# Batch 0's output product made whole instead of from half-size block products, with a new table of ranks

## The chip, the cores and the metric

One core of a Trainium2 chip runs the whole program. The metric is the time of one execution on the device, in microseconds. The engines are named as the profile names them: PE (TensorE matmul), PEld (its weight loads), DVE (VectorE), ACT (ScalarE), POOL (GpSimd), SP (SyncE, which issues every DMA here).

## What is computed

Eight batches of banded attention (8 heads, 576 positions, head size 64) feed a gated layer with spatial mixing. Cut to what matters:

```python
attn = softmax(scale * q @ k.T, masked to a band of 32, or of 128 at every 4th place)   # per head
x    = (attn @ v) with the heads side by side                     # 576 x 512 per batch
h    = relu(x @ w_in);  u, v = h[..., :512], h[..., 512:]
v_n  = (v - mean(v)) / sqrt(var(v) + 1e-6)
v_s  = einsum('ts,bsd->btd', w_spatial, v_n) + b_spatial
out  = (u * v_s) @ w_out                                          # the output product
```

## The kernel before

**Numbers in two parts.** Operands of the large products are split into a high and a low part (names ending in `h` and `l`), and a product is three passes: high by high, high by low, low by high (`PASSES`, line 272). A product of 128x128 by 128x288 over 512 inputs is then 4 x 3 = 12 matmuls.

**Stages of a batch.** `unit` (line 452) makes the scores of two head pairs, 24 small matmuls on parts of the array (line 465 in the trace, 48 records each), the softmax on DVE, ACT and POOL, and three transposes on PE (line 513) that ACT copies out (line 516). `weighted` (line 521) multiplies by the values (line 541, small matmuls too). `features_in` (line 574) splits the result. `v_tile` (line 592) makes the v half (lines 610 and 624) and normalises it. `gate` (line 697) makes the spatial product (lines 707 to 709) and multiplies it by u (DVE, line 714).

**Half-size block products.** The u half (from batch 1 on; batch 0's is made whole by `upper`, line 677, since `FU` is 1 at line 674) and the output product (in every batch) are not made whole. Both operands are cut in 2x2 blocks, and seven products of blocks replace eight: `differences` (line 803) makes differences of right-hand blocks on POOL (line 817), `factor` (line 771) splits seven right-hand blocks into high and low (ACT, line 790; DVE, line 276 through the helper `sub`), `summed` (line 735) makes sums and differences of the weight blocks once (POOL, lines 743 and 745; DVE, lines 748 to 754; ACT, line 765; DVE again through `sub`), and `piece` (line 845) makes each of the seven products in two halves `m` (6 matmuls each, line 827) and adds them up on DVE (line 868, or an ACT copy, line 870, for the first). So a batch's output product is 7 x 2 x 6 = 84 matmuls, and a whole one would be 8 x 12 = 96.

**The order of the work** is set while the program is built. Every function above is a generator that yields what it needs and the engine it wants next; `Timeline` (line 26) holds them with a rank each, keeps a modelled time of every engine, and at each step issues the instruction whose modelled start plus a small share of its rank is least (`run`, line 102). Small matmuls late in the program may be held back by up to 0.5 (`HOLD`, line 40) unless the one before was small too. The ranks come from formulas in the batch loop plus the table `shift` (line 926). `warm` (line 886) fills PE with dummy matmuls (line 891) whenever the modelled time is under 30 and nothing else is ready. Engines then run their queues strictly in that order.

**Start.** SP loads in the order of the list `first` (line 912). Each of the eight chunks of `w_in` and four of `w_out` arrives in 64-bit form and is converted by `weight` (line 296): ACT, four DVE steps, and a last sum made on PE (lines 331 to 333, then an ACT copy), on POOL or on DVE, as the table `ways` says (line 900).

Of the kernel before, what the change touches and what calls it, by code (L numbers as in the profile page):

```python
# [25 lines left out]
class Timeline:  # L26
# [13 lines left out]
    HOLD, HELD = 0.5, 0.5  # L40

# [23 lines left out]
    def start(self, s):  # L65
# [21 lines left out]
        s.wished = start + self.HOLD if small and not self.tiled else 0.0  # L87
# [14 lines left out]
    def run(self):  # L102
        W = 0.05
        while self.strands:
            best = None
            for s in list(self.strands):
                start = self.start(s)
                if start is None:
                    continue
                key = max(start, s.wished) + (W if start > 60 else 0.05) * s.rank[0]  # L110
                if best is None or key < best[2] - 1e-9:
                    best = (start, s, key)
# [31 lines left out]
def tile_banded_attention_gated_moe(  # L144
# [151 lines left out]
    def weight(key, hi, lo, dtype, how):  # L296
# [23 lines left out]
        tl.add(-0.15 + key[-1] * 0.01, rounded(hi, g, ("hi", *key)))  # L320
# [353 lines left out]
    FU = 1  # L674
# [58 lines left out]
    def summed(kind, i):  # L733
# [37 lines left out]
    def factor(b, kind, name, source):  # L771

        def needs(i):
            if len(name) == 1:
                return [("diff", b, kind, int(name), i)] + [("part", b, kind, "2", i)] * (name == "4")
            return [("g", b, *source(i))] + [("diff", b, kind, 2, i)] * (name == "22")

        yield needs(0)
        if kind == "u":
            yield [("fac", b - 1, "o", n) for n in ("11", "21", "1", "2", "3", "22", "4")]  # L780
        yield "fac"
        for i in range(2):
# [11 lines left out]
            if kind == "o" and name in ("3", "22", "4"):  # L794
# [89 lines left out]

    def warm():
# [14 lines left out]
    ways = ((POOL, PE, DVE, PE), (PE, PE, PE, PE), (PE, PE, DVE, PE))  # L900
    halves = {}
    for half in (1, 0):
        cols = slice(half * NF, half * NF + NF)
        for c in range(NC):
# [4 lines left out]
            r = -1.72 + 0.11 * c if half else -2.6 + 0.02 * c  # L909
# [4 lines left out]
        heads_in(0, 1, 1, NU), heads_in(0, 0, 1, NU), halves[1, 2], heads_in(0, 3), spatial_in(4), values_in(0, 0),  # L914
        halves[1, 3], halves[0, 3], halves[0, 2], values_in(0, 1), halves[1, 1], outs[2],
# [5 lines left out]
    for c in range(NC):  # L921
        tl.add(-1.46 + 0.36 * c, weight(("wo", c), wo[0][:, c, :], wo[1][:, c, :], w_out.dtype, ways[2][c]))
    for c in range(5):
        tl.add(1.56 if c < 4 else -0.79, spatial(c))
    tl.add(-0.15, bias())
    shift = {
        ("differences", 0): 0.6,
        ("differences", 1): 0.07,
        ("differences", 2): -0.22,
        ("differences", 3): 0.46,  # L930
        ("factor", 0): 0.18,
        ("factor", 1): 0.18,
        ("factor", 2): -0.33,
        ("factor", 3): -0.03,
        ("factor", 4): -0.26,
# [5 lines left out]
        ("factor", 10): -0.3,  # L941
        ("features_in", 0): -0.23,
        ("features_in", 1): 0.15,
        ("features_in", 2): -0.06,
# [3 lines left out]
        ("gate", 2): 0.07,  # L948
# [7 lines left out]
        ("piece", 0): 1.19,  # L956
# [3 lines left out]
        ("piece", 5): -0.72,  # L960
        ("piece", 6): -0.3,
        ("piece", 7): 0.07,
        ("piece", 8): 0.66,
# [3 lines left out]
        ("piece", 12): -0.11,  # L967
        ("piece", 14): 0.1,
        ("piece", 16): -0.37,
        ("piece", 17): -0.1,  # L970
# [4 lines left out]
        ("piece", 22): -0.52,  # L975
# [13 lines left out]
        ("values_in", 1): 0.3,  # L989
        ("values_in", 2): 0.15,  # L990
        ("values_in", 3): 0.01,
        ("weighted", 0): -0.21,
        ("weighted", 1): -0.52,
# [3 lines left out]
    def put(rank, strand):  # L997

        turn = turns[strand.__name__] = turns.get(strand.__name__, -1) + 1
        tl.add(rank + (shift.get((strand.__name__, turn), 0.0) if b else 0.0), strand)  # L1000

    for b in range(B):
        turns = {}
        AO, AS = (-0.7, 0.7) if b == 1 else (0.15, 0.65)
# [19 lines left out]
        for n, (name, source) in enumerate(  # L1024
            (("11", far(0, 0)), ("21", far(1, 0)), ("1", far(0, 0)), ("2", far(0, 0)), ("3", far(0, 1)), ("22", far(1, 1)), ("4", far(1, 0)))
# [4 lines left out]
        for i in range(2):  # L1030
            put(b + 0.75 + 0.01 * i, differences(b, "o", i))
# [92 lines left out]
```

## Time and profile before

| | |
|---|---|
| runs | 550.97, 550.05, 547.73 us; median 550.05 |
| the profiled execution | 547.6 us, with a span of 545.8 us (the rest, 1.8 us, lies around the span) |
| mean granted TensorE clock | 0.999 of full speed |
| PE busy | 536.9 us, 98% of the span |
| DVE busy | 437.6 us, 80% |
| ACT, POOL busy | 306.8 us, 56%; 213.8 us, 39% |

How to read it: the busy time of PE is the union of its matmul records, whose ends are modelled, so that the spacing of their starts tells more than their durations. A start that comes late shows in the idle time before it and in what released it. The profiled execution is the fastest of the four; the sums of the prediction are made against it.

### The profile page before, as it was taken

How to read it: one execution, taken by the hardware profiler on the slowest of the kernel's cores; microseconds unless marked ns; L12 is line 12 of the kernel's file. 1: busy time of each engine (PE TensorE's matmuls, PEld its weight loads, DVE VectorE, ACT ScalarE, POOL GpSimd, SP SyncE). 2: the span in 40 equal slices, each digit the busy share in tenths (PEclk: the TensorE clock that was granted, in tenths of full speed). 3: DMA queues.
4: the chain of work that ended last, by engine and by line, in shares of the span. 5: the costliest groups of instructions: out<-in, count | busy, mean ns of one | idle time of the engine just before them, and what ended most of it. 6: DMA issues, size and time to landing. Idle time of an engine off the chain costs nothing.

```text
span 545.8 us, 18357 instructions
## 1 busy us (share of the span) xinstructions
PE 536.9 (98%) x7591; PEld 488.1 (89%) x7591; DVE 437.6 (80%) x1036; ACT 306.8 (56%) x939; POOL 213.8 (39%) x255
## 2 busy tenths in 40 slices
PE   9998999999999999999999999999999999999997
PEld 7666789989999899988999999989999899989996
DVE  5888968999957898489957998489957999479836
ACT  4777796555654555556464655556464565454312
POOL 3320275453517163434427163343417163353140
PEclk9999999999999999999999999999999999999999
DMA  8999551201563144411464134521454134201002
GB/s 235 256 175 328 168 124 53 85 11 45 128 139 125 44 133 90 125 67 56 112 131 138 44 106 95 133 80 49 118 118 150 45 116 91 63 12 44 34 1 87
DMA packets 97447, 56.66 MB, mean 104 GB/s; under 512 B 78290, under 2 KB 87506, under 8 KB 97364
## 3 DMA queue, kind: packets, MB, share of 16 engines
q1 hardware_dynamic: 97364, 55.50, 38.1%
q8 instruction: 59, 0.97, 0.8%
q14 instruction: 24, 0.20, 0.1%
HBM read 46.04 MB, written 9.44 MB: 102 GB/s over the span
## 4 chain that ended last, share of the span: by engine, by line
PE 95%; ACT 2%; DMA 1%; issue 1%; DVE 1%; SPq 0%
PE bank L827 32%; PE bank L707 19%; PE bank L610 16%; PE bank L541 6%; PE bank L465 6%; PE bank L891 4%; PE bank L513 3%; PE bank L624 2%; PE bank L686 2%; PE bank L709 2%; PE bank L708 2%; DMA kqv<-in_vw_dram 1%; PE bank L331 1%; ACT p L493 1%; PE bank L332 0%
## 5 line engine op out<-in xcount | busy, mean ns | idle before, releaser
L868 DVE TENSOR_TENSOR ur<-ur,bank 128x288 f32<-128x288 f32 x210 | 87.3, 447 | 27.1 <-PE bank L827 26.8
L790 ACT CAST fac<-ur 128x288 fp32r<-128x288 f32 x112 | 46.2, 430 | 78.4 <-DVE ur L714 42.2
L707 PE MATMUL bank<-wth,vnh 128*128 128x288 f32 x256 | 76.5, 299 | 0.0
L276 DVE TENSOR_TENSOR fac<-ur,fac 128x288 fp32r<-128x288 f32 x112 | 60.5, 549 | 19.1 <-ACT fac L790 18.9
L707 PE MATMUL bank<-wth,vnl 128*128 128x288 f32 x256 | 75.6, 295 | 0.0
L707 PE MATMUL bank<-wtl,vnh 128*128 128x288 f32 x256 | 75.6, 295 | 0.0
L817 POOL TENSOR_TENSOR ur<-ur,ur 128x288 f32<-128x288 f32 x64 | 55.3, 874 | 44.4 <-DVE ur L714 34.0
L493 ACT ACTIVATE p<-p,nm 128x64 f32<-128x64 f32 x192 | 64.5, 338 | 12.5 <-DVE nm L487 10.1
L508 POOL TENSOR_TENSOR p<-p,rv 128x384 f32<-128x384 f32 x48 | 40.7, 850 | 77.1 <-DVE rv L506 61.0
L646 POOL TENSOR_TENSOR rs<-rs,halfneg 128x1 f32<-128x1 f32 (+1 forms) x40 | 27.9, 698 | 91.2 <-DVE rs L644 91.1
L827 PE MATMUL bank<-fac,woh 128*128 128x288 f32 x256 | 53.4, 298 | 0.1
L610 PE MATMUL bank<-wih,xl 128*128 128x512 f32 x128 | 50.1, 392 | 1.8 <-issue 1.8
L817 POOL TENSOR_TENSOR raw<-raw,raw 128x288 f32<-128x288 f32 x42 | 43.4, 1040 | 19.3 <-DVE fac L276 16.4
L610 PE MATMUL bank<-wih,xh 128*128 128x512 f32 x128 | 50.4, 394 | 0.0
L610 PE MATMUL bank<-wil,xh 128*128 128x512 f32 x128 | 50.3, 393 | 0.0
L707 PEld LDWEIGHTS bank<-wth,vnh 128*128 128x128 f32 x256 | 48.2, 188 | 0.4
L707 PEld LDWEIGHTS bank<-wth,vnl 128*128 128x128 f32 x256 | 48.1, 188 | 0.2 <-issue 0.2
L707 PEld LDWEIGHTS bank<-wtl,vnh 128*128 128x128 f32 x256 | 48.2, 188 | 0.0
L714 DVE SCALAR_TENSOR_TENSOR ur<-ur,bank 128x288 f32<-128x288 f32 x64 | 27.9, 448 | 21.1 <-PE bank L709 20.5
L827 PEld LDWEIGHTS bank<-fac,woh 128*128 128x128 f32 x256 | 42.2, 189 | 2.6 <-ACT raw L568 0.4
L827 PE MATMUL bank<-fac,o 128*128 128x288 f32 x288 | 44.0, 297 | 0.0
L827 PEld LDWEIGHTS bank<-fac,o 128*128 128x128 f32 x288 | 40.6, 188 | 1.6
(155 smaller groups left out, 1368.4 us busy)
## 6 DMA issues: line engine op xcount, KB each, us to landing
kqv<-in_vw_dram SPq DMA_DIRECT2D x128, 144.0 KB, 3.7
out_dram<-ur SPq DMA_DIRECT2D x64, 144.0 KB, 1.8
kqv<-in_kT_dram SPq DMA_DIRECT2D x30, 304.0 KB, 4.2
kqv<-in_qT_dram SPq DMA_DIRECT2D x30, 288.0 KB, 3.6
kqv<-in_w_in_dram SPq DMA_DIRECT2D x16, 256.0 KB, 5.6
kqv<-in_w_out_dram SPq DMA_DIRECT2D x4, 512.0 KB, 8.6
kqv<-in_w_spT_dram SPq DMA_DIRECT2D x5, 288.0 KB, 6.2
kqv<-in_kT_dram SPq DMA_DIRECT2D x2, 192.0 KB, 4.5
```

What stands on the lines that cost most here:

```text
L276: nc.vector.tensor_sub(out, a, b.bitcast(F32))
L465: nc.tensor.matmul(s[j][q * QB : q * QB + QB, e, :], kq[r, WIN + S :].rearrange("p (u n i t) -> p u t n i", n=2, i=QB, t=US)[:, u, g // 2 ...
L493: nc.scalar.activation(p[:, e, j], p[:, e, j], AF.Exp, bias=nm[:, i : i + 1], accum_out=sm[:, i : i + 1])
L508: nc.gpsimd.tensor_mul(flat, flat, rv.unsqueeze(2).broadcast_to([P, 2 * US, KW]))
L541: nc.tensor.matmul(acc[j][1][1][i * D : i * D + D, (g - h * HB) * QB : (g - h * HB + 1) * QB], v[r, g, :], probs[b, G, u][1][r, e, q * QB ...
L610: nc.tensor.matmul(pm, x[c][a][:, cols], wi[w][:, c, NF:], start=c == 0 and n == 0, stop=c == NC - 1 and n == 2)
L646: nc.gpsimd.tensor_tensor(rs[:m], rs[:m], halfneg[:m], op=ALU.pow)
L707: nc.tensor.matmul(pv, vn[c][a][:, fs], wt[w][:, c, ts], start=n == 0, stop=False)
L790: nc.scalar.copy(dst[:, 0, i, :], src)
L817: nc.gpsimd.tensor_sub(at(*to), at(*a), at(*c))
L827: nc.tensor.matmul(bank[:, :HS], left(i, w)[:, m * P : m * P + P], right, start=n == 0, stop=n == 5)
L868: op(ob[1], mine[src][1], bank[:, :HS])
```

## The change

1. **Batch 0's output product whole.** With `FO = 1` a new generator, `whole`, makes each of batch 0's eight 128x288 output tiles with 12 matmuls (line 900 of the changed kernel) and one ACT copy. For batch 0 only four factors are split (blocks 11, 21, 12, 22), and `differences` and the additions of `piece` fall away.
2. **The sums of output weight blocks behind it.** `summed("o", i)` now also waits for all eight tiles, since it overwrites a part of `w_out`.
3. **One chunk of w_out** is finished on DVE instead of PE (`ways`).
4. **Planner rules.** A small matmul group is now held until nine such groups could start or 0.5 has passed (`NEED`), and gets a bonus of 0.1 while small matmuls are running (`STICK`).
5. **Ranks and load order.** `first` brings a chunk of `w_in` ahead of the rest of the first heads; `shift` is changed in some places, and two further tables, `second` (batch 1) and `first` (batch 0), are added.

```diff
     HOLD, HELD = 0.5, 0.5
+    NEED, STICK = 9, 0.1
...
-        s.wished = start + self.HOLD if small and not self.tiled else 0.0
+        s.small = start if small else None
...
+            can = [(start, s) for start, s in ((self.start(s), s) for s in list(self.strands)) if start is not None]
+            small = sorted(start for start, s in can if s.small is not None)
+            enough = small[self.NEED - 1] if len(small) >= self.NEED else float("inf")
+            for start, s in can:
+                key = start
+                if s.small is not None:
+                    key = start - self.STICK if self.tiled else max(start, min(enough, s.small + self.HOLD))
+                key += (W if start > 60 else 0.05) * s.rank[0]
...
-    FU = 1
+    FU, FO = 1, 1
...
+        else:
+            yield [("whole", b, h, m) for b in range(FO) for h in range(2) for m in range(4)]
         yield "mid mid"
...
+    def whole(b, h, m):
+
+        yield [("fac", b, "o", name) for name in (("11", "21"), ("12", "22"))[h]]
+        yield [("wo", c) for c in range(NC)]
+        yield "mm bank ur"
+        *held, ob = yield PE, 1.6
+        po = held[1][1][:, :HS]
+        for n, (f, (w, a)) in enumerate(itertools.product(range(NC), PASSES)):
+            right = facs[b, "o", (("11", "21"), ("12", "22"))[h][f // 2]][1][:, a, f % 2, :]
+            nc.tensor.matmul(po, wo[w][:, f, m * P : m * P + P], right, start=n == 0, stop=n == 3 * NC - 1)
+        tl.done("whole", b, h, m)
+        if all(("whole", b, h, i) in tl.time for i in range(4)):
+            tl.give(*(facs[b, "o", name] for name in (("11", "21"), ("12", "22"))[h]))
+        yield ACT, 0.3, 0.1
+        nc.scalar.copy(ob[1], po)
...
+        nc.sync.dma_start(out[b, m * P : m * P + P, h * HS : h * HS + HS], ob[1])
...
-    ways = ((POOL, PE, DVE, PE), (PE, PE, PE, PE), (PE, PE, DVE, PE))
+    ways = ((POOL, PE, DVE, PE), (PE, PE, PE, PE), (DVE, PE, DVE, PE))
...
-        heads_in(0, 1, 1, NU), heads_in(0, 0, 1, NU), halves[1, 2], heads_in(0, 3), spatial_in(4), values_in(0, 0),
-        halves[1, 3], halves[0, 3], halves[0, 2], values_in(0, 1), halves[1, 1], outs[2],
+        heads_in(0, 1, 1, NU), halves[1, 2], heads_in(0, 0, 1, NU), heads_in(0, 3), spatial_in(4), values_in(0, 0),
+        halves[0, 3], halves[0, 2], halves[1, 3], values_in(0, 1), halves[1, 1], outs[2],
...
+    second = {
...
+    first = {
...
+        key = strand.__name__, turn
+        rank += shift.get(key, 0.0) + second.get(key, 0.0) * (b == 1) if b else first.get(key, 0.0)
+        tl.add(rank, strand)
...
+        for n, (h, m) in enumerate(itertools.product(range(2), range(4))):
+            if b < FO:
+                put(b + 0.9 + 0.06 * n, whole(b, h, m))
...
-                    if kind == "o" or b >= FU:
+                    if b >= (FO if kind == "o" else FU):
...
-        tl.add(0.65, summed("o", i))
-        tl.add(0.7, summed("u", i))
+        tl.add(0.28, summed("o", i))
+        tl.add(0.85, summed("u", i))
```

The first place is PE's queue at batch 0's output product. Before, products of weight sums (`o`) stand there, each of 6 matmuls into a bank:

```order
L610 MATMUL bank_64<-wih,xh_165 128x512
L610 MATMUL bank_64<-wil,xh_165 128x512
L610 MATMUL bank_64<-wih,xl_166 128x512
L827 MATMUL bank_68<-fac_1384,o_914 128x288 x6
L827 MATMUL bank_70<-fac_1384,o_914 128x288 x6
```

In the changed kernel a tile of the product is 12 matmuls into one bank, from two factors and the plain weights `woh` and `wol`:

```order
L713 MATMUL bank_64<-wb,vb 128x288
L900 MATMUL bank_71<-fac_1428,woh 128x288 x2
L900 MATMUL bank_71<-fac_1428,wol 128x288
L900 MATMUL bank_71<-fac_1429,woh 128x288 x2
L900 MATMUL bank_71<-fac_1429,wol 128x288
L900 MATMUL bank_70<-fac_1428,woh 128x288 x2
```

Over the whole program PE has 12 more matmuls of this shape, six more dummies and one final weight sum (lines 331 to 333) less.

The second place is DVE's queue at batch 1's first u factors (`fac<-raw`). Before, additions of batch 0's output product (line 868) and batch 1's v tiles (`vnl`) stand between them:

```order
L868 TENSOR_TENSOR ur_107<-ur_107,bank_68 128x288
L276 TENSOR_TENSOR fac_1405<-raw_95,fac_1405 128x288
L276 TENSOR_TENSOR vnl_116<-mid_85,vnh_115 128x512
L868 TENSOR_TENSOR ur_108<-ur_108,bank_70 128x288
L868 TENSOR_TENSOR ur_103<-ur_103,bank_67 128x288
L868 TENSOR_TENSOR ur_104<-ur_104,bank_65 128x288
```

In the changed kernel the sums of output weight blocks stand there (`mid`, `o` and `wol`):

```order
L758 TENSOR_TENSOR mid_86<-mid_87,mid_86 128x256
L280 TENSOR_TENSOR o_1043<-mid_88,o_1043 128x256
L760 TENSOR_TENSOR mid_87<-mid_87,mid_86 128x256
L280 TENSOR_TENSOR fac_1430<-raw_95,fac_1430 128x288
L280 TENSOR_TENSOR o_1045<-mid_85,o_1045 128x256
L280 TENSOR_TENSOR o_1044<-mid_87,o_1044 128x256
L280 TENSOR_TENSOR fac_1430<-raw_96,fac_1430 128x288
L280 TENSOR_TENSOR wol<-mid_85,woh 128x256
L280 TENSOR_TENSOR o_1044<-mid_87,o_1044 128x256
L280 TENSOR_TENSOR fac_1428<-raw_95,fac_1428 128x288
```

So the same factors now queue behind the sums that before had been made ahead of batch 0's output product.

The third place is PE's queue ahead of the second value product (`pT`) of a later batch. Before, nothing but a spatial product and block products precede it for a while:

```order
L709 MATMUL bank_69<-wb,vb 128x288
L827 MATMUL bank_71<-fac_1384,wih 128x288 x2
L827 MATMUL bank_71<-fac_1384,wil 128x288
L541 MATMUL bank_64<-pT_92,kqv_76 64x32
```

In the changed kernel the last three transposes of the same heads (`plus,p`) stand only 12 matmuls ahead of it, in each batch from the second on:

```order
L517 MATMUL bank_71<-plus,p_91 128x128 x3
L833 MATMUL bank_67<-fac_1428,woh 128x288 x2
L833 MATMUL bank_67<-fac_1428,wol 128x288
L833 MATMUL bank_68<-fac_1430,woh 128x288 x2
L833 MATMUL bank_68<-fac_1430,wol 128x288
L545 MATMUL bank_64<-pT_92,kqv_76 64x32
```

The copy that ACT makes of these transposes is what the value product reads first. In the whole of the program, PE changes from large to small matmuls (of the scores and values) 58 times before and 56 times after.

## Rows read from the trace of the kernel before

**Rows 1.** The head of the profile page and its first part: busy time, share of the span, instructions.
```profile
span 545.8 us, 18357 instructions
PE 536.9 (98%) x7591; PEld 488.1 (89%) x7591; DVE 437.6 (80%) x1036; ACT 306.8 (56%) x939; POOL 213.8 (39%) x255
```

**Rows 2.** The table of stretches: from and to in us, length, then busy time of PE, PEld, DVE, ACT and POOL with the count of instructions, granted clock, DMA share and GB/s. The first is batch 0's gated stage and batch 1's start, the second a later batch, the third a part of the last batch with almost nothing but matmuls of 288 columns.
```profile
95.60:156.20 60.60, 60.59 (x666) 56.31 (x665) 56.75 (x140) 33.96 (x112) 27.68 (x31) 1.00 0.28 77
218.20:280.00 61.80, 61.80 (x935) 57.40 (x936) 49.88 (x120) 34.64 (x110) 24.89 (x29) 1.00 0.37 99
500.00:530.00 30.00, 30.00 (x221) 29.60 (x221) 19.88 (x47) 8.43 (x20) 9.57 (x11) 1.00 0.06 21
```

**Rows 3.** The chain that ended last, in order of time (start, us, what): the first value product of the second and of the sixth batch after the start.
```profile
156.26 2.23 PE bank L541 x144
...
465.38 2.23 PE bank L541 x144
```

**Rows 4.** Who PE waited for over the whole span: the waiting line, the releaser, us in total, times, longest. "issue" is a wait for nothing that the profile shows.
```profile
PE bank L610 <- issue: 1.8, 1, 1.8
PE bank L465 <- issue: 0.9, 1, 0.9
PE bank L332 <- ACT wih L352: 0.5, 1, 0.5
PE bank L541 <- issue: 0.4, 1, 0.4
PE bank L465 <- ACT mid L616: 0.3, 1, 0.3
PE bank L827 <- issue: 0.3, 1, 0.3
```

**Rows 5.** PE's timeline (start, us, line, out<-in, shape, count) in the last batch, products back to back.
```profile
537.31 3.34 PE L827 MATMUL bank<-fac,o 128*128 128x288 f32 x24
540.49 0.42 PE L827 MATMUL bank<-fac,woh 128*128 128x288 f32 x2
```

**Rows 6.** PE's timeline at the start: dummies, and what follows them.
```profile
25.81 2.79 PE L891 MATMUL bank<-vnl 128*128 128x512 f32 x11
28.44 0.49 PE L513 MATMUL bank<-plus,p 128*128 128x128 f32 x3
```

**Rows 7.** PE's timeline at one final weight sum of `w_out`, and the matmul behind it.
```profile
59.02 1.06 PE L331 MATMUL bank<-kqv,plus 128*128 128x512 f32 x2
59.50 0.81 PE L332 MATMUL bank<-woh,minus 128*128 128x512 f32 x1
60.15 0.39 PE L333 MATMUL bank<-wol,plus 128*128 128x512 f32 x1
60.38 0.40 PE L610 MATMUL bank<-wih,xh 128*128 128x512 f32 x1
```

**Rows 8.** PE's timeline around one group of scores (48 records) and around two groups in one (96), each followed by six block products.
```profile
142.62 0.29 PE L709 MATMUL bank<-wb,vb 97*128 97x288 f32 x1
142.84 0.76 PE L465 MATMUL bank<-kqv 64*32 64x64 f32 x48
143.53 1.07 PE L827 MATMUL bank<-fac,u 128*128 128x288 f32 x6
144.43 0.49 PE L513 MATMUL bank<-plus,p 128*128 128x128 f32 x3
...
179.78 1.27 PE L465 MATMUL bank<-kqv 64*32 64x64 f32 x96
180.98 1.07 PE L827 MATMUL bank<-fac,o 128*128 128x288 f32 x6
181.88 0.39 PE L610 MATMUL bank<-wih,xh 128*128 128x512 f32 x1
```

**Rows 9.** The costliest groups of instructions (line, engine, operation, out<-in, shapes, count, then busy us and mean ns, and the idle time before): the additions of block products, the ACT and DVE halves of a factor, and the differences.
```profile
L868 DVE TENSOR_TENSOR ur<-ur,bank 128x288 f32<-128x288 f32 x210 | 87.3, 447 | 27.1 <-PE bank L827 26.8
L790 ACT CAST fac<-ur 128x288 fp32r<-128x288 f32 x112 | 46.2, 430 | 78.4 <-DVE ur L714 42.2
L276 DVE TENSOR_TENSOR fac<-ur,fac 128x288 fp32r<-128x288 f32 x112 | 60.5, 549 | 19.1 <-ACT fac L790 18.9
L817 POOL TENSOR_TENSOR ur<-ur,ur 128x288 f32<-128x288 f32 x64 | 55.3, 874 | 44.4 <-DVE ur L714 34.0
```

**Rows 10.** PE's timeline at the one late start in the last batch.
```profile
532.10 0.43 PE L827 MATMUL bank<-fac,woh 128*128 128x288 f32 x2
532.37 0.29 PE L827 MATMUL bank<-fac,wol 128*128 128x288 f32 x1
532.50 0.87 PE L827 MATMUL bank<-fac,woh 128*128 128x288 f32 x2
```

**Rows 11.** The timeline at three transposes (PE, line 513) and ACT's queue after them.
```profile
90.39 0.49 PE L513 MATMUL bank<-plus,p 128*128 128x128 f32 x3
90.89 0.67 ACT L583 CAST xh<-raw 128x576 fp32r<-128x576 f32 x1
91.46 0.48 ACT L516 COPY pT<-bank 128x384 f32<-128x384 f32 x1
```

**Rows 12.** DVE's timeline in the sums of output weight blocks, and POOL's at the same place.
```profile
83.75 1.40 DVE L752 TENSOR_TENSOR mid<-mid,mid 128x256 f32<-128x256 f32 x1
...
101.59 0.42 DVE L748 TENSOR_TENSOR mid<-mid,mid 128x256 f32<-128x256 f32 x1
...
102.84 0.42 DVE L276 TENSOR_TENSOR o<-mid,o 128x256 fp32r<-128x256 f32 x1
...
83.40 1.46 POOL L743 TENSOR_TENSOR mid<-woh,wol 128x512 f32<-128x512 f32 x1
```

More of the change, by code (lines that the diff above doesn't have):

```diff
@@ L793, in factor @@
             tl.done("part", b, kind, name, i)
-            if kind == "o" and name in ("3", "22", "4"):
+            if kind == "o" and (name in ("3", "22", "4") or b < FO):
                 tl.give(raw[(b,) + source(i)])
@@ L883, in piece @@
         tl.give(*held)
+    def whole(b, h, m):
[12 more added lines that the diff above has]
+        nc.scalar.copy(ob[1], po)
+        tl.give(*held)
+        tl.done("out", b, h, m)
+        if all(("out", b, i, n) in tl.time for i in range(2) for n in (m % 2, m % 2 + 2)):
+            tl.done("made", b, "o", m % 2, "1w")
+        nc.sync.dma_start(out[b, m * P : m * P + P, h * HS : h * HS + HS], ob[1])
+        now = tl.now
+        tl.now += 2.5
+        tl.give(ob)
+        tl.now = now
     def warm():
@@ L947, in tile_banded_attention_gated_moe @@
         ("gate", 1): -0.16,
-        ("gate", 2): 0.07,
+        ("gate", 2): 0.14,
         ("gate", 3): -0.18,
@@ L955, in tile_banded_attention_gated_moe @@
         ("heads_in", 3): -0.33,
-        ("piece", 0): 1.19,
+        ("piece", 0): 1.12,
         ("piece", 1): -0.04,
@@ L974, in tile_banded_attention_gated_moe @@
         ("piece", 21): -0.45,
-        ("piece", 22): -0.52,
+        ("piece", 22): -0.49,
         ("piece", 23): -0.87,
@@ L988, in tile_banded_attention_gated_moe @@
         ("values_in", 0): 0.22,
-        ("values_in", 1): 0.3,
         ("values_in", 2): 0.15,
-        ("values_in", 3): 0.01,
-        ("weighted", 0): -0.21,
-        ("weighted", 1): -0.52,
+        ("values_in", 3): -0.02,
+        ("weighted", 0): 0.09,
+        ("weighted", 1): -0.37,
+    }
+    second = {
+        ("differences", 0): 0.07,
+        ("differences", 1): -0.15,
+        ("differences", 2): 0.3,
+        ("factor", 0): -0.3,
+        ("factor", 1): 0.03,
+        ("factor", 2): 0.33,
+        ("factor", 4): -0.07,
+        ("factor", 5): -0.15,
+        ("factor", 8): 0.03,
+        ("factor", 10): -0.37,
+        ("features_in", 1): -0.3,
+        ("features_in", 3): 0.07,
+        ("gate", 3): -0.07,
+        ("heads_in", 1): -0.15,
+        ("piece", 1): -0.03,
+        ("piece", 8): -0.15,
+        ("piece", 16): -0.33,
+        ("piece", 18): -0.03,
+        ("piece", 21): 0.07,
+        ("piece", 23): -0.3,
+        ("piece", 25): 0.03,
+        ("piece", 26): 0.07,
+        ("piece", 27): -0.18,
+        ("unit", 0): 0.07,
+        ("upper", 0): 0.15,
+        ("v_tile", 0): 0.03,
+        ("v_tile", 1): 0.07,
+        ("values_in", 1): -0.15,
+        ("values_in", 3): 0.03,
+        ("weighted", 0): -0.07,
+    }
+    first = {
+        ("factor", 6): 0.3,
+        ("features_in", 1): 0.15,
+        ("features_in", 2): -0.3,
+        ("features_in", 3): -0.15,
+        ("gate", 0): -0.07,
+        ("gate", 2): -0.3,
+        ("gate", 4): 0.03,
+        ("gate", 6): -0.07,
+        ("piece", 3): -0.3,
+        ("piece", 4): -0.07,
+        ("piece", 7): -0.3,
+        ("piece", 9): 0.03,
+        ("piece", 12): 0.3,
+        ("unit", 0): -0.15,
+        ("unit", 3): -0.07,
+        ("unit", 4): 0.03,
+        ("upper", 3): -0.07,
+        ("v_tile", 4): -0.07,
+        ("weighted", 0): 0.03,
+        ("weighted", 1): 0.15,
+        ("whole", 0): 0.04,
+        ("whole", 5): -0.3,
+        ("whole", 6): 0.3,
+        ("whole", 7): -0.07,
     }
```

59 lines of the change are left out of this document (28 added, 31 removed).

## The prediction

> **What bounds the kernel now.** The head of the page comes first: PE is busy for 536.9 of 545.8 us, DVE for 80%, the others for less [rows 1]. That alone settles nothing, since the ends of matmuls are modelled, so the table of stretches comes next. In a later batch PE is busy for 61.80 of 61.80 us while DVE has 12 us to spare, and in batch 0's gated stage, where the change takes work away, PE is busy for 60.59 of 60.60 us beside a DVE at 56.75 [rows 2]. The chain of waits says the same in another way: the first value product comes at 156.26 us in one batch and at 465.38 us five batches later, so 61.8 us a batch [rows 3], and PE stands on the chain throughout. The reader is to see that from about 60 us on the time is the sum of what PE has to issue, plus the few moments at which it stands still. Those are listed in the waits of PE: 0.8 us behind ACT, and 3.4 us in four pauses for which the profile names no producer [rows 4]. One more shows only in the timeline: two matmuls that take 0.87 us where the two before took 0.43, so 0.44 us near the end [rows 10]. Together 4.6 us, under 1% of the span. This is all that a better order can give while the work on PE stays what it is.
>
> So the change has to be counted on PE, instruction by instruction, since every engine runs its queue in order and the dummies are instructions like any other.
>
> **The change, part by part.**
>
> *The whole product on PE.* It takes 96 matmuls instead of 84. Of the same shape 24 start within 540.49 - 537.31 = 3.18 us, so 0.1325 us each [rows 5]. Twelve more cost +1.59 us. Nothing hides them: PE is the engine that is full.
>
> *What it saves beside PE.* By the text of `piece`, 14 additions on DVE go (7 for each half), at 0.447 us 6.3 us; by `factor`, 3 of 7 factors, so 6 casts of ACT at 0.430 and 6 subtractions of DVE at 0.549, 2.6 and 3.3 us; by `differences`, 8 subtractions of POOL at 0.874, 7.0 us [rows 9]. ACT gets eight copies in place of two. I cost all this at nothing. The cover is PE's own queue in that stage [rows 2]: DVE's 9.6 us were already hidden behind it, so their going away uncovers nothing. If that cover were thinner than it looks, the saving would count; that is a rival below.
>
> *The final sum of one chunk of w_out.* From its start to the matmul behind it PE spends 60.38 - 59.02 = 1.36 us [rows 7]. One goes: -1.36 us. Its work comes back as two subtractions and additions on DVE, ahead of the gated stage, in place of one copy of ACT.
>
> *Dummies.* Eleven of them take 28.44 - 25.81 = 2.63 us, so 0.24 each [rows 6]. The changed order holds six more: +1.43 us. They stand where the first heads' loads now arrive behind a chunk of w_in. SP issues the same transfers in another order, and the bytes up to the last weight are the same, so I price the order of loads by these dummies alone.
>
> *Fewer turns to small matmuls.* One group of scores enters 142.84 - 142.62 - 0.13 = 0.09 us late and runs with six products behind it for 144.43 - 142.84 = 1.59 us; without the products' 6 x 0.1325 = 0.80 that is 0.88 us in all. Two groups in one take 181.88 - 179.78 - 0.80 + 0.09 = 1.39 us [rows 8], so a turn saved is worth 2 x 0.88 - 1.39 = 0.37 us. The order has 56 turns instead of 58: -0.74 us. In the later batches the number is unchanged, seven in each, so the new planner rules give nothing there and the 61.8 us of a batch stay.
>
> *The sums of output weight blocks.* They are made once in either kernel and cost PE nothing; what matters is what stands behind them on DVE. They now stand among batch 1's first u factors, which PE soon needs. From the first combination shown there to the last of these factors some seven of their operations lie ahead, where before about four additions did. At 0.42 us for one in quiet moments [rows 12] against 0.447 [rows 9] that is 7 x 0.42 - 4 x 0.447 = 1.15 us more. The lower bound is 0 (a part of a v tile has left the same place, and DVE may be ahead there); the upper one is the row in which the same operation took 1.40 us beside POOL's addition [rows 12], 7 x 1.40 - 1.8 = 8 us. I take 0.5 us, near the quiet rows, because POOL's four additions come first and most of the subtractions follow when they are over.
>
> *Transposes close ahead of the value product.* The cover of ACT's copy shrinks to 12 matmuls, 1.6 us, in each later batch. The copy took 0.48 us and waited 0.57 us for a cast in front of it; from the first transpose to the copy's end were 91.46 + 0.48 - 90.39 = 1.55 us [rows 11], of which the transposes themselves overlap nothing of the 12. I cost this at nothing, narrowly: with a second cast in front PE would wait some 0.5 us a batch.
>
> *The moments at which PE stands still.* The 0.8 us behind ACT [rows 4] come from a place in the start that is ordered anew, and the 0.44 us [rows 10] from products that started before their factors were split; in the changed order all of the last batch's spatial products run first. I let these 1.24 us go. The four pauses without a producer have no cause that I could remove. Three of them, 3.1 us, fall before 96 us, where the order is new. Between all staying (0) and all going (-3.4) I take half, -1.7 us, for want of a nearer row.
>
> *Sum.* 1.59 + 1.43 - 1.36 - 0.74 = +0.92 us of work on PE; -1.24 for named waits, -1.7 for pauses, +0.5 for the sums: -1.5 us. Against the profiled execution, 547.6 us, that is 546.1 us. That execution is 2.45 us under the median of the runs, 550.05, and I carry the difference over to it: 548.5 us.
>
> **A rule that speaks for more.** In the stage in question PE's weight loads are busy for 56.31 of 60.60 us, while in a stretch of nothing but products they are for 29.60 of 30.00 [rows 2]. The Trainium skill ("Perfetto Trace Analysis", section "Identifying the Most-Contended Engine") says that matmul occupancy misleads and that the weight loads' share is the measure of headroom. By that rule PE would have 60.60 - 56.31 = 4.29 us to spare in this stage, and the sum would be -5.8 us. I don't follow it here. The small matmuls and those of 512 columns also leave the weight loads idle without PE waiting for anyone, and the waits of PE in that stage are near nothing [rows 4].
>
> **The rivals.**
>
> 1. *All standing still goes.* If the new order of the start removes every pause and wait and the sums cost nothing, 0.92 - 4.64 = -3.7 us: 546.3 us. For it: the pauses sit in the part that is rearranged. Against: they name no engine, so no order addresses them.
> 2. *PE was held by DVE after all* in batch 0's gated stage, and the stage shortens by the 60.60 - 56.31 = 4.29 us in which no weight is being loaded [rows 2]: -1.5 - 4.3 = -5.8 us: 544.2 us. For it: DVE at 56.75 of 60.60 us there. Against: no wait for it.
> 3. *Work alone.* The waits and pauses turn up elsewhere in the same size: +0.9 us, 551.0 us. For it: a pause without a producer has no reason to shrink.
> 4. *The sums come too late.* PE waits at batch 1's u products, because the four combinations of the first pair run beside POOL's additions (1.46 us each) at 1.40 instead of 0.42 us [rows 12]: 4 x 0.98 = 3.9 us on DVE ahead of the factors. With the named waits gone and the pauses unmoved, 0.92 + 3.9 - 1.24 = +3.6 us: 553.6 us. It decides as soon as DVE is later there than the some 7 us of products that PE has in hand (52 matmuls from the first u product of batch 1 to the first that needs such a factor). Against: DVE loses 9.6 us of work before that point.
>
> **How the numbers follow.** A difference under 0.5%, 2.75 us, can't be told from none in a measurement of this kernel. The forecast, -1.5 us, has 0.48; rival 1 0.18; rival 2 0.07; rival 3 0.14; rival 4 0.13. Faster by over 0.5% are rivals 1 and 2: 0.25. Within it are the forecast and rival 3: 0.62. Slower is rival 4: 0.13. The range leaves out rivals 2 and 4, 0.2 together, and reaches from a little under rival 1 to beyond rival 3 with the sums at their quiet price and one cast too many in the later batches: 545.4 to 552.8 us.
>
> **What would show it.** In the profile after: matmuls of 288 columns at the same 0.13 us; 96 of them in the whole product; a later batch again at 61.8 us between value products; DVE less busy in batch 0's stage with PE no sooner through it. Wrong would be: a wait of PE for DVE at batch 1's u products (rival 4), a batch shorter or longer than 61.8 us (the transposes or the planner rules), or a gated stage shorter by more than what goes on PE (rival 2). If PE's idle time is as before, rival 3 holds.

## The result: slower by 1.4%

The changed kernel takes 555.49 us (median of five runs, 554.44 to 557.55) against 548.72 us of the kernel before on the same chip (546.78 to 550.97): a ratio of 1.0137, 95% interval 1.0119 to 1.0156. The forecast was 548.5 us with a range up to 552.8. The place is that of rival 4. Its mechanism, combinations that run beside POOL, is about half of what happened there (below), and the time is 1.9 us above its price.

The profiled execution of the changed kernel took 555.5 us, with this head of the page (engine, busy us, share, instructions), against [rows 1]:

```profile
span 553.7 us, 18339 instructions
PE 540.0 (98%) x7605; PEld 492.2 (89%) x7605; DVE 424.3 (77%) x1018; ACT 305.6 (55%) x938; POOL 202.3 (37%) x247
```

The span grew by 7.9 us, PE's busy time by 3.1, and DVE and POOL lost 13.3 and 11.5 us of work without anybody gaining from it. The table of stretches of the changed kernel, against [rows 2] (from and to, length, busy time of PE, PEld, DVE, ACT, POOL with counts, granted clock, DMA share, GB/s):

```profile
95.60:130.00 34.40, 34.40 (x351) 31.80 (x350) 25.06 (x60) 13.31 (x31) 7.25 (x9) 1.00 0.10 34
130.00:160.00 30.00, 26.15 (x320) 24.52 (x307) 27.24 (x67) 18.58 (x74) 14.86 (x15) 0.94 0.26 70
232.20:293.80 61.60, 61.60 (x935) 57.51 (x936) 48.45 (x120) 34.40 (x110) 23.77 (x30) 1.00 0.36 99
500.00:530.00 30.00, 30.00 (x200) 28.47 (x199) 22.41 (x55) 10.00 (x22) 6.60 (x9) 1.00 0.06 21
```

The reader is to see that the first, third and fourth stretch are as full as before, and that the second is not: PE is busy for 26.15 of 30.00 us there, and the clock's mean is 0.94. A later batch still takes 61.6 us from value product to value product (the chain in order of time, against [rows 3]):

```profile
232.24 2.23 PE bank L545 x144
...
293.80 2.23 PE bank L545 x144
```

Who PE waited for, in the changed kernel, against [rows 4] (line, releaser, us in total, times, longest):

```profile
PE bank L833 <- DVE fac L280: 3.4, 3, 2.4
PE bank L517 <- POOL p L512: 2.2, 2, 1.1
PE bank L711 <- issue: 1.2, 1, 1.2
PE bank L922 <- DVE vnl L225: 1.0, 1, 1.0
PE bank L545 <- issue: 1.0, 1, 1.0
PE bank L545 <- ACT pT L520: 0.5, 1, 0.5
PE bank L614 <- issue: 0.4, 1, 0.4
PE bank L833 <- issue: 0.4, 1, 0.4
PE bank L469 <- issue: 0.3, 1, 0.3
```

The two at the top, behind DVE and POOL, are new. The one of L922 is the first dummy's, at 1.04 us; the kernel before has it too, at its line 891 (1.0 us), beside those of [rows 4]. PE's timeline of the changed kernel at the two places inside 130 to 160 us (start, us, line, out<-in, shape, count, idle time before and its releaser):

```profile
138.95 0.55 PE L517 MATMUL bank<-plus,p 128*128 128x128 f32 x3 [1.10 <-POOL p L512]
...
147.11 0.29 PE L833 MATMUL bank<-fac,u 128*128 128x288 f32 x1
149.78 0.67 PE L833 MATMUL bank<-fac,u 128*128 128x288 f32 x3 [2.38 <-DVE fac L280]
150.82 2.29 PE L833 MATMUL bank<-fac,u 128*128 128x288 f32 x8 [0.37 <-DVE fac L280]
```

The first u product of batch 1 that needs a split difference starts its high pass at 147.11 us and then waits for the low part, which DVE makes. DVE's timeline says why it is late:

```profile
141.43 1.50 DVE L754 TENSOR_TENSOR mid<-mid,mid 128x256 f32<-128x256 f32 x1
142.96 1.40 DVE L756 TENSOR_TENSOR mid<-mid 128x256 f32<-128x256 f32 x1
144.39 0.94 DVE L758 TENSOR_TENSOR mid<-mid,mid 128x256 f32<-128x256 f32 x1
145.36 0.94 DVE L760 TENSOR_TENSOR mid<-mid,mid 128x256 f32<-128x256 f32 x1
...
148.94 0.42 DVE L760 TENSOR_TENSOR mid<-mid,mid 128x256 f32<-128x256 f32 x1
149.27 0.45 DVE L280 TENSOR_TENSOR fac<-raw,fac 128x288 fp32r<-128x288 f32 x1
```

From 141.43 us to the factor at 149.27 us DVE does almost nothing but sums of output weight blocks, ten operations of them. The first four take 4.78 us in place of some 1.7. POOL's timeline shows what runs beside them: the second pair's additions beside the first two, and two softmax operations that had queued behind the additions beside the other two:

```profile
141.35 1.30 POOL L749 TENSOR_TENSOR mid<-woh,wol 128x512 f32<-128x512 f32 x1
142.60 1.48 POOL L751 TENSOR_TENSOR mid<-woh,wol 128x512 f32<-128x512 f32 x1
144.04 1.01 POOL L504 TENSOR_TENSOR p<-p,nm 128x384 f32<-128x384 f32 x1
145.01 1.01 POOL L512 TENSOR_TENSOR p<-p,rv 128x384 f32<-128x384 f32 x1
```

**The whole difference on PE, by place.** Charge every matmul what it takes from start to start in undisturbed rows (0.1325 us for 288 columns [rows 5], a turn to small matmuls 0.37 [rows 8], the others likewise), and what is left over is standing still or running slowly; the dummies are counted with it. Worked out in this way from all starts of PE:

| stretch, us | before | after | parted sums (below) |
|---|---|---|---|
| 0 to 80 | 28.00 | 28.16 | 28.35 |
| 80 to 130 | 0.76 | 2.46 | 3.18 |
| 130 to 145 | 0.32 | 1.21 | 1.22 |
| 145 to 180 | 0.02 | 4.72 | 0.26 |
| 180 to 520 | 1.00 | 1.54 | 1.65 |
| 520 to the end | 0.47 | 1.31 | 1.30 |

Turns (-0.74) and charged work (+0.24) added, the changed kernel's last matmul comes 8.3 us later, and 0.4 us less lies behind it. Over half of it is one place.

### The profile page after: what moved, and what is told of

Same layout as the page of the kernel before. It is cut to its first block, busy times and chain, and to the rows that moved or that the text cites. A ratio compares the mean times of both kernels' runs of the same rounds, so it can differ in the third digit from the quotient of the medians.

```text
span 553.7 us, 18339 instructions
## 1 busy us (share of the span) xinstructions
PE 540.0 (98%) x7605; PEld 492.2 (89%) x7605; DVE 424.3 (77%) x1018; ACT 305.6 (55%) x938; POOL 202.3 (37%) x247
## 4 chain that ended last, share of the span: by engine, by line
PE 88%; DVE 6%; ACT 2%; issue 1%; DMA 1%; POOL 1%; SPq 0%; ACTq 0%; DVEq 0%
PE bank L833 28%; PE bank L711 18%; PE bank L614 15%; PE bank L545 6%; PE bank L469 5%; PE bank L517 3%; PE bank L628 3%; PE bank L690 2%; PE bank L922 2%; PE bank L713 2%; PE bank L712 1%; DVE kqv L323 1%; PE bank L900 1%; ACT p L497 1%; PE bank L335 1%
## 5 line engine op out<-in xcount | busy, mean ns | idle before, releaser
L874 DVE TENSOR_TENSOR ur<-ur,bank 128x288 f32<-128x288 f32 x196 | 81.5, 446 | 14.3 <-PE bank L833 12.4
L796 ACT CAST fac<-ur 128x288 fp32r<-128x288 f32 x106 | 44.1, 437 | 76.8 <-DVE ur L718 47.2
L512 POOL TENSOR_TENSOR p<-p,rv 128x384 f32<-128x384 f32 x48 | 43.1, 899 | 80.8 <-DVE rv L510 71.1
L823 POOL TENSOR_TENSOR ur<-ur,ur 128x288 f32<-128x288 f32 x56 | 46.7, 840 | 44.4 <-DVE ur L718 33.6
L650 POOL TENSOR_TENSOR rs<-rs,halfneg 128x1 f32<-128x1 f32 (+1 forms) x40 | 29.1, 728 | 79.0 <-DVE rs L648 78.7
L823 POOL TENSOR_TENSOR raw<-raw,raw 128x288 f32<-128x288 f32 x42 | 34.9, 836 | 47.2 <-DVE fac L280 39.5
L833 PE MATMUL bank<-fac,woh 128*128 128x288 f32 x224 | 46.8, 299 | 0.0
L280 DVE TENSOR_TENSOR xl<-raw,xh 128x576 fp32r<-128x576 f32 x32 | 29.4, 936 | 17.3 <-ACT xh L587 17.3
L545 PEld LDWEIGHTS bank<-pT,kqv 64*64 64x64 f32 x2304 | 35.5, 135 | 5.5 <-issue 3.9
L545 PE MATMUL bank<-pT,kqv 64*64 64x32 f32 x2304 | 37.9, 220 | 1.5 <-issue 1.0
```

The source lines that it names most:

```text
L280: nc.vector.tensor_sub(out, a, b.bitcast(F32))
L512: nc.gpsimd.tensor_mul(flat, flat, rv.unsqueeze(2).broadcast_to([P, 2 * US, KW]))
L545: nc.tensor.matmul(acc[j][1][1][i * D : i * D + D, (g - h * HB) * QB : (g - h * HB + 1) * QB], v[r, g, :], probs[b, G, u][1][r, e, q * QB ...
L650: nc.gpsimd.tensor_tensor(rs[:m], rs[:m], halfneg[:m], op=ALU.pow)
L796: nc.scalar.copy(dst[:, 0, i, :], src)
L823: nc.gpsimd.tensor_sub(at(*to), at(*a), at(*c))
```

## The experiments

Theory A is that the sums of output weight blocks, where they now stand, hold up DVE in front of batch 1's u factors. Against it stand B (the merged score groups and the new order do it), C (the sums would be in the way anywhere) and D (the new ranks and rules cost the time, not the whole product). The line numbers of rows are those of the kernel that was run. The edits are shortened, and lines with # say in words what stands there.

The first five are judged by one stretch in which PE's order does not change: from the start of the 144 score records at 128.37 us to the second value product behind them. In the changed kernel it is 174.72 - 128.37 = 46.35 us:

```profile
128.37 1.78 PE L469 MATMUL bank<-kqv 64*32 64x64 f32 x144
...
174.72 2.30 PE L545 MATMUL bank<-pT,kqv 64*64 64x32 f32 x144
```

### The sums earlier

```diff
 def summed("o", i):
-    # adds, combinations, roundings and corrections behind the eight tiles of `whole`
+    # the same instructions as soon as the sums for u are done; block 3 into room of its own
```

> The changed kernel with one move and nothing else: the 4 additions on POOL, the 8 combinations on DVE and the 8 roundings and 8 corrections that make the sums of output weight blocks stand right behind the sums for u (about 104 to 117 us) and no longer behind batch 0's whole product; the third sum has room of its own, so the whole product still reads the unsummed block. PE's order is untouched. Theory A (the sums, where they stand now, hold DVE and POOL in front of batch 1's u factors, and PE's wait takes its clock down): the waits of 2.38 + 0.37 us at 149.8 us and of 1.10 us at 138.95 us go and the 1.7 us of the low clock with them, 5.5 us in all, so 555.5 becomes 550.0 (549 to 551.5). Theory B (the waits there come from the merged score groups and the re-tuned order, the sums only stand beside them): the two waits stay, 554 to 556. Theory C (the sums would be in the way wherever they stand): a new wait of PE of over 2 us shows between 105 and 135 us, 552 to 556.

Besides, to make room, the edit lowers the buffers of the softmax's row values from 6 to 3 and of the v tiles' from 4 to 3. What that alone does was not run.

Measured: 553.09 us (552.78 to 554.51), ratio 1.0085 (1.0054 to 1.0116), and 44.24 us for the stretch. The waits at 147 us are gone, and theory B falls for them. But the time is not A's 549 to 551.5, and C is right here: all of DVE's 18 operations in a row now end at 119.6 us, and DVE's last gate of batch 0 and batch 1's v tiles come that much later (in the changed kernel the gate ran at 112.54 and the v tile's sum at 116.60 us):

```profile
119.38 0.29 DVE L281 TENSOR_TENSOR minus<-mid,u 128x128 fp32r<-128x128 f32 x1
119.58 0.45 DVE L719 SCALAR_TENSOR_TENSOR ur<-ur,bank 128x288 f32<-128x288 f32 x1
120.11 0.68 DVE L637 TENSOR_TENSOR mid<-mid,bank 64x512 f32<-64x512 f32 x1
```

PE pays for it with 0.57 and 1.43 us in front of the whole product's second half, whose factors wait in the same queue.

### The sums later

```diff
 def summed("o", i):
-    # behind the eight tiles of `whole`, at once
+    # POOL's additions behind batch 1's last fast u product, the rest in two steps behind its gates
```

> The changed kernel with the same instructions of the sums moved the other way: behind batch 1's u products, spread over about 157 to 172 us, where DVE and POOL were busy for half of the time or less; their first reader, an output product of batch 1, stands near 185 us. PE's order and everything else is untouched. Theory A: as for the early place, both waits and the low clock go, 550.0 (549 to 551.5). Theory B: the waits stay, 554 to 556. Theory C: PE waits for DVE or ACT between 157 and 190 us instead, 552 to 556.

Measured: 552.69 us (551.32 to 553.36), ratio 1.0072 (1.0048 to 1.0097), 43.13 us for the stretch. The time lies in C's range again. PE no longer waits between 140 and 154 us. A new wait of 0.84 us comes at 155.94 us, and DVE's timeline shows it as the same collision, now with a factor of the output product: its low part takes 1.53 us where 0.45 is usual, while POOL's additions run from 152.83 to 158.28 us.

```profile
154.36 1.53 DVE L280 TENSOR_TENSOR fac<-ur,fac 128x288 fp32r<-128x288 f32 x1
```

The wait of 1.10 us behind POOL at 138.7 us stayed in both runs. My expectation that it would go with the sums was wrong: POOL's additions stand behind that multiply, not ahead of it.

### Dummies across the wait

```diff
 def product(bank, b, kind, m, left, name):
+    if (b, kind, name) == (1, "u", "2"):        # its first half m
+        for n in range(19):
+            nc.tensor.matmul(bank[:, :HS], plus, wa[:, :HS], start=True, stop=True)
```

> The changed kernel with 19 more dummy matmuls of 288 columns (19 x 0.1325 = 2.5 us) on PE just ahead of batch 1's u product that waits at 147.1 to 149.8 us, into the bank that this product then overwrites; nothing else moved. It separates the wait from the clock. Theory A: PE works through the wait, its granted clock stays at 1.0 from 150.5 to 153.9 us, and the 1.7 us that the 3.41 us at half speed cost come back: 553.8 (553.2 to 554.5). If the fall of the clock has another reason, or costs nothing since the factors are late anyway: 555.5 (555 to 556).

Measured: 554.74 us (553.82 to 556.15), ratio 1.0109 (1.0080 to 1.0137), which can't be told from the changed kernel's. The clock did what was expected. The table of stretches, first of the changed kernel, then with the dummies:

```profile
145.00:149.70 4.70, 2.40 (x19) 2.16 (x17) 4.60 (x13) 2.07 (x6) 1.02 (x2) 1.00 0.00 0
...
150.50:153.90 3.40, 3.08 (x13) 3.08 (x14) 3.40 (x10) 1.15 (x3) 0.00 (x0) 0.50 0.00 0
```

```profile
145.00:149.30 4.30, 4.30 (x34) 4.30 (x34) 4.20 (x12) 1.96 (x6) 0.73 (x1) 1.00 0.00 0
...
150.50:153.90 3.40, 2.74 (x18) 2.51 (x19) 3.37 (x10) 1.16 (x3) 0.00 (x0) 1.00 0.00 0
```

The stretch to the second value product is 46.36 us, that is, not a hundredth better:

```profile
128.08 1.78 PE L469 MATMUL bank<-kqv 64*32 64x64 f32 x144
...
174.44 2.30 PE L545 MATMUL bank<-pT,kqv 64*64 64x32 f32 x144
```

So the clock of 0.50 for 3.4 us cost nothing. DVE is full in both (3.40 and 3.37 of 3.40 us), and PE at full clock only waits for the next factors instead (PE busy 2.74 of 3.40). My 1.7 us were counted on the wrong engine. The profiled execution is 0.8 us shorter than the changed kernel's, and it lacks a pause of 0.97 us (the one at 305 us, below).

### POOL's additions left out

```diff
-        nc.gpsimd.tensor_add(w[0], w_[0][:, i, :], w_[1][:, i, :])
+        if kind == "u":
+            nc.gpsimd.tensor_add(w[0], w_[0][:, i, :], w_[1][:, i, :])
...                                             # and the second addition likewise
```

> The changed kernel with the 4 additions on POOL of the sums of output weight blocks left out (the combinations on DVE then work on what the buffers held before, so the output of batches 1 to 7 is not the reference's); every other instruction stands where it stood. It parts the two ways in which the sums can hold DVE up: their 16 operations in its queue at 0.42 us each, or the 4 of them that took 1.50, 1.40, 0.94 and 0.94 us beside POOL. If it is what DVE loses beside POOL's 512-wide additions: the 4 combinations take 0.42 to 0.45 us, DVE comes to batch 1's u factors 3.1 us earlier, PE's 2.38 + 0.37 us at 149.8 us and the low clock behind them go, 551 to 552. If the number of operations ahead of the u factors is what counts: the wait shrinks by under 1 us, 554.5 to 555.5.

Measured: 553.61 us (552.67 to 554.95), ratio 1.0094 (1.0061 to 1.0127), 43.93 us for the stretch, 2.4 less than in the changed kernel. The whole time's interval overlaps that of the changed kernel, so this run is read from the stretch. Both halves of the explanation count. Of the first four combinations three fall to their quiet time, and the first, beside one softmax operation of POOL, takes 0.96 us (DVE's timeline):

```profile
141.80 0.96 DVE L756 TENSOR_TENSOR mid<-mid,mid 128x256 f32<-128x256 f32 x1
142.79 0.43 DVE L758 TENSOR_TENSOR mid<-mid 128x256 f32<-128x256 f32 x1
143.25 0.42 DVE L760 TENSOR_TENSOR mid<-mid,mid 128x256 f32<-128x256 f32 x1
143.71 0.42 DVE L762 TENSOR_TENSOR mid<-mid,mid 128x256 f32<-128x256 f32 x1
```

That is worth 2.4 us. PE still loses 0.53, 0.78 and 0.61 us ahead of its starts at 148.81, 151.28 and 157.98 us by the spacing of its starts, since the sums remain ahead of the factors in DVE's queue. The time came out between the two expectations.

### The sums parted

```diff
 def summed("o", i):
-    # i = 0 and 1 behind the eight tiles of `whole`
+    # i = 0 behind batch 0's last gate, its block 3 into room of its own
+    # i = 1 behind batch 1's gates
```

> The changed kernel with its sums of output weight blocks parted: the first half (2 additions on POOL, 4 combinations, 4 roundings and 5 corrections) right behind batch 0's last gate product, about 113 to 117 us, the second half (2 additions, 4 combinations, 4 roundings and 4 corrections) behind batch 1's u products, about 159 to 167 us; PE's order untouched. The early place of all of them left PE waiting 0.22 + 0.57 + 1.43 us for the factors of the whole product (130 to 134 us), the late place 0.84 us at 155.94 us beside POOL's additions and 1.4 us between 170 and 180 us. Theory A (any place costs what it pushes back, and half the load fits into the idle time of DVE at either): those 2.2 to 2.7 us go too, while the 1.10 us behind POOL at 138.7 us stays: 550.3 (549.3 to 551.5). If what is left has another source than where the sums stand: 552 to 553.5.

Measured: 551.68 us (551.10 to 552.12), ratio 1.0049 (1.0033 to 1.0065), and the stretch is 171.17 - 129.34 = 41.83 us, 4.5 less than in the changed kernel:

```profile
129.34 1.78 PE L469 MATMUL bank<-kqv 64*32 64x64 f32 x144
...
171.17 2.30 PE L545 MATMUL bank<-pT,kqv 64*64 64x32 f32 x144 [0.36 <-ACT pT L520]
```

From 145 to 180 us PE now loses 0.26 us in place of 4.72 (table above), with the same instructions on every engine but two operations more. DVE's timeline shows it standing idle, waiting for PE, where it was the bound:

```profile
141.84 0.55 DVE L491 TENSOR_REDUCE nm<-p 128x6 f32<-128x384 f32 x1
143.76 0.45 DVE L950 TENSOR_TENSOR ur<-ur,bank 128x288 f32<-128x288 f32 x1 [1.36 <-PE bank L909]
```

Theory A holds for this place. The time ended 1.4 us above the 550.3 expected, just outside the range. A part of that stands between 80 and 130 us, where PE loses 3.18 against 2.46 us; the rest isn't traced. By the median it is also the best of these kernels, and still slower than the kernel before.

### Whole product or ranks: four corners

```diff
-    FU, FO = 1, 1        # the changed kernel
+    FU, FO = 1, 0        # no whole product, new ranks and rules
```

> The changed kernel with its one switch for the whole product set back (batch 0's output made by block products again, the sums made ahead of them), with the new ranks, order of loads and rules of the planner kept. Theory A (the whole product's late sums cost the time): near the kernel before, 547 to 550.5. Rival D (the new ranks, load order and rules cost it): 553 to 557.

```diff
-    FU = 1               # the kernel before
+    FU, FO = 1, 1        # with whole(), the sums' wait and the four factors; old ranks and rules
```

> The kernel before with the whole product of batch 0 and the sums' wait for it, and nothing else of the change: old ranks, old order of loads, old planner rules. Theory A (the sums behind the whole product cost the time, whatever the ranks): slower than the kernel before by 4 to 9 us, 553 to 557, with PE waiting for DVE's u factors of batch 1 and a low clock behind it. Rival D (the new ranks and rules cost it): 547 to 550.

> The same as the whole product alone on the kernel before, with its sums parted as in the parted run of the changed kernel (half behind batch 0's last gate, half behind batch 1's u products), PE's order as in the whole product alone. Theory A: 3 to 6 us less than the whole product alone, since the waits for batch 1's u factors go. Rival D: the same time as the whole product alone within 0.7 us.

| | no whole product | whole product | whole, sums parted |
|---|---|---|---|
| old ranks, loads, rules | 548.9 | 568.19 (ratio 1.0361, 1.0332 to 1.0391) | 560.28 (1.0209, 1.0192 to 1.0226) |
| new ranks, loads, rules | 558.29 (1.0171, 1.0146 to 1.0196) | 555.49 (1.0137, 1.0119 to 1.0156) | 551.68 (1.0049, 1.0033 to 1.0065) |

Both one-sided expectations missed: the whole product with the old ranks costs 19 us, beyond A's 4 to 9, and the new ranks without it cost 10, beyond D's range. The new ranks cost 9.4 us without the whole product and save 12.7 with it, so ranks are worth only what they are worth in the order for which they were chosen, and these corners don't decide between A and D for the whole difference. What both rows of the table share is the place. Without the whole product, PE waits for no factor at batch 1's u products under the new ranks either. With the old ranks PE's timeline has the same two waits:

```profile
151.36 0.67 PE L829 MATMUL bank<-fac,u 128*128 128x288 f32 x3 [2.63 <-DVE fac L276]
152.77 2.29 PE L829 MATMUL bank<-fac,u 128*128 128x288 f32 x8 [0.74 <-DVE fac L276]
```

and with the sums parted PE has none there (table of stretches):

```profile
145.00:160.00 15.00, 15.00 (x157) 14.76 (x156) 10.92 (x30) 5.41 (x21) 5.50 (x6) 1.00 0.37 78
```

where the whole product alone had 11.63 of 15.00 us at a clock of 0.89. With the old ranks parting the sums saves 7.9 us, more than the 3 to 6 expected and than the 3.4 us of these two waits; where the rest comes from isn't traced. Another part of what the old ranks lose is six waits of 1.2 us on average, one in a later batch each time, of a v tile for the last split feature (7.3 us in all). They stay with the sums parted (7.7 us), and their cause is open.

### The other wait

```diff
 def unit(b, G, u):
+        if n == (2, 0, 0):
+            yield [("prod", 1, "u", "11", 1)]
         yield "pt bank pT"
```

This is the kernel with the parted sums and one need more.

> The changed kernel with the parted sums, and batch 2's transposes of pairs 0 and 1, third group of queries counted from the end (they stood waiting for POOL's multiply for 1.10 us at 138.7 us) put behind batch 1's first u product for the other row half, as a need of that one request in the planner; PE's order within batch 1 changes with it. If the wait is only a matter of what stands in front of the transposes: 1.0 us less than the parted sums, 550.7 (550.2 to 551.3), and the wait of 1.1 us for POOL gone. If the softmax of the merged score groups is late for PE in any case: the wait moves to another place and the time stays at 551.2 to 552.2.

Measured: 556.80 us (556.20 to 557.77), ratio 1.0151 (1.0126 to 1.0175). The wait at 138.7 us is gone, and two others behind the same multiply stand a batch later:

```profile
271.61 0.55 PE L519 MATMUL bank<-plus,p 128*128 128x128 f32 x3 [1.18 <-POOL p L512]
273.05 0.55 PE L519 MATMUL bank<-plus,p 128*128 128x128 f32 x3 [0.89 <-POOL p L512]
```

One need in the planner's input moved batches that it doesn't name. Of the second expectation the wait's move came true; the time didn't stay at 551.2 to 552.2 but rose to 5.1 us above the parted sums. So this run doesn't tell what the wait at 138.7 us costs.

## Why the prediction was wrong

**What bounds the kernel.** Right for all but one stretch: PE is full at 34.40 of 34.40, 61.60 of 61.60 and 30.00 of 30.00 us. From 141 to 160 us DVE's queue was the bound: DVE was busy for 18.63 of 19.00 us and PE for 16.25. With the sums parted it is the other way round, 13.25 and 19.00 us.

**The base.** 2.45 us were carried over from the profiled execution of 547.6 us to the median of the runs; in the runs beside the changed kernel that median was 548.72, so 1.3 us of the forecast were too much, in the direction that hid a part of the miss.

**Work on PE.** +1.59 - 1.36 was predicted for the twelve matmuls and the one weight sum, and the charged work rose by 0.24. The price of 0.1325 us held, and nothing hid it.

**Dummies**, +1.43: right in size (97 in place of 91, 25.94 us against 24.32), and offset on the spot. Up to 80 us dummies and standing still sum to 28.16 us, against 28.00: the pauses there shrank to 0.4 us from 2.7 and the wait for ACT went, while a first wait of 1.1 us behind POOL came at 44 us.

**Turns**, -0.74: the 56 turns are there. The price of one was charged here as forecast, not measured again.

**The sums of output weight blocks**, +0.5: the step that failed. They cost 4.7 us between 145 and 180 us, of which parting them returns 4.5; of the 4.5 some 2.4 are the collision with POOL's additions and with the softmax operations that they push back, and the rest is their number in the queue. The prediction had both rows and chose between them by an argument on order ("POOL's four additions come first and most of the subtractions follow when they are over"). The first pair's combinations need only the first two additions, so they run beside the second two. The near row was the 1.40 us one of [rows 12], not the quiet one. It also counted seven operations ahead of the factors, from the piece of the order that it showed, where ten stand ahead of the first that PE waited for. The upper bound of 8 us was written down and then left out of the range.

**"DVE loses 9.6 us of work before that point"**, the argument against rival 4, is true and doesn't help. DVE stood idle for 1.96 and 3.61 us around 112 to 116 us in the changed kernel, while the sums, by their new need, could not begin before the whole product was done. Work that goes ahead of a need can't be spent behind it.

**The moments of standing still**, -1.24 and -1.7. The late start near the end came back in another place (PE's timeline of the changed kernel, against [rows 10]):

```profile
542.89 0.79 PE L833 MATMUL bank<-fac,o 128*128 128x288 f32 x4 [0.61 <-DVE fac L280]
```

By the spacing of starts it is 0.88 us against 0.44. Pauses without a producer sum to 3.3 us against 3.4, so next to nothing of the 1.7 came: what went before 80 us stands at 95.44 and 305.41 us now, as rival 3 has it. The wait of 1.10 us behind POOL at 138.95 us is in no term. ACT's and POOL's queues there hold the softmax of three score groups that run in one turn at 128.37 us; that this makes it late is read, not shown. Both belong to the whole product and not to the new ranks and rules: with the whole product, the parted sums and the old ranks PE has the same merged groups and the same wait.

```profile
128.48 1.78 PE L465 MATMUL bank<-kqv 64*32 64x64 f32 x144
...
139.30 0.55 PE L513 MATMUL bank<-plus,p 128*128 128x128 f32 x3 [1.10 <-POOL p L508]
```

Without the whole product, under old ranks or new, no more than two groups (96 records) stand in one turn between 100 and 145 us, and PE doesn't wait for POOL there.

**Transposes close ahead of the value product**, at nothing, and rightly: one wait of 0.5 us in the whole span, at 90.57 us and so in no later batch.

**Rival 2, the rule on weight loads.** PEld is at 31.80 of 34.40 us in batch 0's stage and PE at 34.40, though DVE has fallen to 25.06: there was no headroom to gain.

**Left open.** The parted sums are 2.8 us slower than the kernel before by the medians, and 4.5 us by the spans of the two profiled executions. Of the 4.5 the table puts 2.4 between 80 and 130 us, 0.9 between 130 and 145 us, where the wait behind POOL stands, and 0.8 at the end, less the turns saved. Why PE stands still longer between 80 and 130 us isn't shown. The wait behind POOL at 44 us and the one of 0.6 us near the end come with the new ranks and order of loads: every run with them has both, with the whole product or without, and no run with the old ones has either.

## What to carry to other kernels

When a change adds a need to setup work, look for where it now lands in every queue, and price it by the busiest row of the same operation, not by the quiet one, unless the order rules out the collision instruction by instruction. Work saved ahead of the need is no cover for it. And before a low clock is counted, ask who is full while it lasts: the slow PE behind a full DVE cost nothing here.

## What was not expected of the hardware

**PE's pauses follow instruction loads.** The pauses named "issue" come just after a transfer of the kind "instruction". In the changed kernel there are 60 such packets (0.98 MB) on a queue of their own. One starts at 93.10 us and takes 0.94, and PE's next matmul comes 1.40 us after its end:

```profile
95.44 0.29 PE L711 MATMUL bank<-wth,vnh 128*128 128x288 f32 x1 [1.18 <-issue]
```

Another ends at 303.92 us, and the matmul behind that pause starts at 305.41; in the kernel before one ends at 50.76, and the matmul starts at 52.09. It is so in all eleven profiles: each of their 55 pauses of this name over 0.15 us ends 1.2 to 1.8 us after such a packet has landed. Most of the packets stop nobody. That the loads are the cause is read from these times; no run moved a load and nothing else.

**DVE beside POOL.** Such an operation on 128x256 took 0.42 us alone, 1.50 and 1.40 beside POOL's 128x512 additions of 1.30 and 1.48, and 0.94 beside POOL's softmax operations of 1.01; with the additions left out three of the four took 0.42 to 0.43. The Trainium skill ("Trainium Architecture — The Big Picture", section "What this means for kernel authors") says that the two engines' shared port pair is held as an exclusive lock and not split. The rows agree: each of the four ends 0.28 us after the POOL operation beside which it started (at 142.93, 144.36, 145.33 and 146.30 us, POOL's at 142.65, 144.08, 145.05 and 146.02), and so does the one of 0.96 us in the run without the additions (142.76 and 142.48).

**The clock.** PE stood still for 2.38 us until 149.78 us, and from 150.50 to 153.90 us the granted clock was 0.50, the lower of its two levels (1.2 of 2.4 GHz). With dummies in the gap it stayed at 1.00.
